# The layer norm's reciprocal root on VectorE (bit trick, two Newton steps) instead of ScalarE (Ln, Exp), with the planner's limits chosen anew

## The chip, the cores and the metric

The kernel runs on one core of one Trainium2 chip. Its engines work side by side and are named as the profile names them: PE (TensorE matmuls; PEld are its weight loads), ACT (ScalarE, the engine with the activation functions), DVE (VectorE), POOL (GpSimd) and SP (SyncE, which here only issues DMAs). The metric is the device time of one execution in microseconds; the median of the runs is compared. A profile is one execution, with every instruction's start and duration.

## The reference

Four layers stand one behind the other on an activation x of 2048 tokens by 512 features; there are 32 heads of 16 features. Layers 0 and 2 are of kind A, layers 1 and 3 of kind B.

```python
x = A_x
x = x + _A_ref(_layernorm(x), A_wq, A_wk, A_wv, A_wo, A_beta)
x = x + _B_ref(_layernorm(x), B_wqkv, B_wo)
x = x + _A_ref(_layernorm(x), A_wq, A_wk, A_wv, A_wo, A_beta)
x = x + _B_ref(_layernorm(x), B_wqkv, B_wo)

def _layernorm(x, eps=1e-05):
    m = mean(x, -1); v = var(x, -1)
    return (x - m) / sqrt(v + eps)
```

Kind A cuts the tokens into four segments of 512. Within a segment it is causal softmax attention; between segments a memory M (16 by 16 for each head) and a norm z are carried, read through phi(q) and written with phi(k), and a gate of beta mixes the two outputs. Kind B is full softmax attention over all 2048 tokens. Each ends in a product with wo and is added to x. So there are 16 normalisations of a segment (four layers by four segments), and in them one reciprocal root for each token: 512 numbers at a time, held as 128 partitions by 4.

## The kernel before

The kernel is laid down by a planner in Python that runs while the program is built. It keeps a model of when each engine will be free and writes the instructions of all five engines in the order that the model finds good; on the chip each engine then follows its own list and waits on semaphores.

**Units.** The main loop (`attention`, `unit`) takes the attention scores in banks of 128 keys by 512 queries, up to three to a unit. PE computes the scores of the banks (`ps<-qm,KB` and `ps<-qm,KA`), and one ACT instruction on line L1925 takes the exponential of all of a unit's banks from PSUM into `pT` in SBUF: 1536 columns for three banks, 1024 for two. PE multiplies `pT` by the values (`ps<-pT,VB`).

**Banks on VectorE.** When the planner thinks that ACT is behind, it gives one or two banks to DVE instead (`dx_open`, `ring_open`, `dx_first`). There an exponential is the sum of three approximations: line L1394 makes a 16-bit integer from the scores in PSUM, whose bits are read as bfloat16, and two more copies are made with an integer added (L1450 for two banks at once, L1493 for four, both on DVE; or L1475 on POOL). PE multiplies all three copies by the values, so a bank on DVE costs three such products and a bank on ACT one. The copies lie in `dxt` and in the buffers `KA`, `QA`, `VA`, `wA` and `wB` while these are not in use for their own data; in rows such as `KA<-ps 128x512 uint16` that name means such a bank.

**Background work.** Normalisations, projections, output products and memory updates are Python generators ("tasks") that the loop advances a step at a time between units. A task yields what it waits for, and how many PE columns and DVE nanoseconds the next step will cost; the loop runs a step when its credit allows it.

**Limits.** Every 20 units `set_limits` sets some 80 numbers from a row of the table `PLAN` (76 rows): from which lag of an engine a bank goes to DVE, when a copy goes to POOL, in which order background steps stand, how many matmuls with zeros are put into gaps of PE (`keep_busy`, `fill_gap`; the rows `ps<-woB,zero`).

**The normalisation** is `ln_part`: for each of a segment's four tiles of 128 tokens DVE computes mean and variance (`bn_stats`, `bn_aggr` into `lnst`). Then ACT makes the reciprocal root of the four variances in two small instructions: Ln with eps as bias on L882 and Exp with scale -0.5 on L885, both into `lnw` (128 by 4). The two are steps of their own; between them lies at least one unit. `normalize` (L895) then subtracts and multiplies on DVE into `xn`, and SP transposes `xn` into `xT` by DMA for the projections. The first segment of all goes through `ln_first` (L906), with transposes on PE and copies out of PSUM by ACT (L920) and DVE.

`setup` loads, before anything else, one activation table that holds both Ln and Exp (L825); Copy and Exp are the only other functions that ACT uses. `evac` copies a projection out of PSUM with DVE, or with ACT (L757) where the planner has ACT ahead of DVE by the limit EVAC_ACT.

Of the kernel before, what the change touches and what calls it, by code (L numbers as in the profile page):

```python
# [5 lines left out]
dt = mybir.dt  # L6
ACT = mybir.ActivationFunctionType
ALU = mybir.AluOpType
# [9 lines left out]
LN_EPS = 1e-5  # L18
LOG2E = 1.4426950408889634
# [397 lines left out]
class Builder:  # L417
# [5 lines left out]
        2: dict(FILL_DVE=400, MASK_PE=800, GAP=3, BG_BANK=400, QMIN=3, LOW=20, POOL_QM=1, ACT1=600, R_PAIRS=2, PE_LOW=7, DX_LATE=1700, DX_FIN=3000, OPART=3, HOLD_AT=12, PE_A=4, NEAR_A=50, TRADE=0, TAKEN_A=1, PART=3, DMA_LATE=700, CR_B=1200, SLACK=350, DMA_STEPS=0, POOL_WAIT=600, MARGIN=250, EVAC_ACT=1500),  # L423
        3: dict(R_LATE=1200, NEARW=40, PAIRS=999, MASK_PE=800, LEVEL=3, TAKEN=0.5, LOW=20, MARGIN=600, TAKEN_A=1, EARLY=300, OPART=3, QUAD=0, FILL=0.47, CR_A=1200, DX_LATE=700, CARRY_W=1500, PART=3, CR_W=2200, HOLD_MAX=0, DVE_LATE=1700, FILL_DVE=400, BUSY_WAIT=500, ACT1=300, QMIN=3, PE_LOW=7, PE_A=6, TRADE=400, DVE_LATE_LOW=2500, PACE=7, PE_B=6, ORD=3, POOL_WAIT=600),
        4: dict(R_LATE=1200, NEARW=40, PAIRS=999, MASK_PE=800, LEVEL=3, TAKEN=0.5, LOW=20, MARGIN=600, TAKEN_A=1, EARLY=300, OPART=0, QUAD=0, FILL=0.47, DX_BANK=900, CR_A=1200, DX_LATE=700, CARRY_W=1500, PART=3, CR_W=2200, HOLD_MAX=0, DVE_LATE=1700, FILL_DVE=400, BUSY_WAIT=500, ACT1=300, QMIN=3, PE_LOW=7, PE_A=6, TRADE=0, DVE_LATE_LOW=2500, POOL_D=2500, PACE=7, PE_B=6, POOL_MEM=0),
        5: dict(ACT1=300, NEAR=8, TAKEN_A=1, PV_SKIP=900, FILL_DVE=400, BACK=8, CR_W=2200, NEARW=40, OPART=0, TAKEN=0.4, LOW=20, DVE_LATE=800, QWAIT=8, HOLD_AT=40, PHI_LATE=0, REST=20, POOL_D=2500, R_LATE=1200, MARGIN=350, EARLY=300, QUAD=0, CR_A=1700, CARRY_W=1500, PART=3, BUSY_WAIT=500, PE_LOW=7, PE_A=6, HURRY=4000, PAIRS=999, LEVEL=3, DX_BANK=900, DX_LATE=700, QMIN=3, TRADE=0, DVE_LATE_LOW=2500, PACE=7, DVE_FIN=1500, MASK_PE=800, FILL=0.47),
        6: dict(ACT1=300, NEAR=8, TAKEN_A=1, PV_SKIP=900, FILL_DVE=400, BACK=8, CR_W=2200, NEARW=40, OPART=0, TAKEN=0.4, LOW=20, DVE_LATE=800, QWAIT=8, HOLD_AT=40, PHI_LATE=0, REST=20, POOL_D=2500, R_LATE=1200, MARGIN=350, EARLY=300, QUAD=0, CR_A=1700, CARRY_W=1500, PART=3, BUSY_WAIT=500, PE_LOW=7, PE_A=6, HURRY=4000, PAIRS=999, LEVEL=3, DX_BANK=900, DX_LATE=700, QMIN=3, TRADE=400, DVE_LATE_LOW=2500, PACE=7, DVE_FIN=1500, MASK_PE=800, FILL=0.47, DMA_LATE=0),
        7: dict(R_LATE=1200, NEARW=40, PAIRS=999, MASK_PE=800, LEVEL=3, TAKEN=0.4, LOW=20, MARGIN=350, TAKEN_A=1, EARLY=300, OPART=0, QUAD=0, FILL=0.47, DX_BANK=900, CR_A=1200, DX_LATE=700, CARRY_W=400, PART=3, CR_W=2200, HOLD_MAX=0, DVE_LATE=800, FILL_DVE=400, BUSY_WAIT=500, ACT1=300, DMA_LATE=0, GAP=3, QWAIT=8, NEAR=8, PE_A=6, POOL_QM=1, DVE_LATE_LOW=2500, PACE=7, DVE_FIN=200, HURRY=1500, PV_SKIP=900, POOL_D=2500, PE_LOW=7, QMIN=3),
        8: dict(R_LATE=1200, NEARW=40, PAIRS=999, MASK_PE=800, LEVEL=3, TAKEN=0.4, LOW=30, MARGIN=500, TAKEN_A=1, EARLY=500, OPART=0, QUAD=0, FILL=0.47, DX_BANK=900, CR_A=1200, DX_LATE=700, CARRY_W=1500, PART=3, CR_W=2200, DVE_LATE=1700, FILL_DVE=400, BUSY_WAIT=500, ACT1=300, DMA_LATE=0, QWAIT=8, NEAR=8, PV_SKIP=900, NEAR_A=0, HURRY=1500, QMIN=3),
        9: dict(MARGIN=600, NEAR=3, PV_SKIP=200, FILL_DVE=100, BUSY_ROOM=900, FILL=0.4, CR_W=1500, CARRY_W=400, R_PAIRS=2, OPART=4, GAP=3, DVE_LATE=800, QMIN=1, HOLD_AT=40, POOL_QM=1, ACT1=300, DX_LATE=900, REST=8, CR_B=1800, DX_LAG=1, BACK=6, LOW=14, BUSY_WAIT=500, POOL_D=1200, PART=3, PHI_LATE=0, EVAC_ACT=100, RUSH0=40, AHEAD=1000, RUSH=120, DX_TAIL=300, FIT=3),  # L430
        10: dict(ACT1=200, MARGIN=600, R_LATE=2200, EVAC_ACT=800, NEAR=10, CR_W=1300, CR_B=1800, R_PAIRS=2, DIV_LATE=800, TAKEN=0.5, DVE_LATE=800, BG_BANK=400, PHI_LATE=300, OPART=3, NEARW=20, POOL_C=2000, DX_LAG=1, POOL_D=1200, REST=12, EARLY=500, POOL_QM=1, DX_FIN=3000, DMA_LATE=1200, PE_LOW=7, HOLD_SEGS=2, PV_SKIP=200, QUAD=0, LN1_AT=6, FILL_DVE=400, QMIN=4, BUSY_WAIT=0, PORT_FREE=150, DX_LATE=700),
        11: dict(ACT1=200, NEAR=10, PV_SKIP=200, EARLY=500, FILL=0.53, CR_B=1800, CARRY_W=400, OPART=2, MASK_PE=800, DIV_LATE=800, BG_BANK=100, QUAD=0, LN1_AT=6, FILL_DVE=400, R_LATE=1500, POOL_C=4000, QMIN=4, POOL_D=1200, DVE_LATE=1700, DX_FIN=3000, POOL_QM=1, DVE_FIN=1500, PE_A=4, SPARE=20, PACE=7, MARGIN=600),
        12: dict(MARGIN=600, NEAR=10, PV_SKIP=100, FILL_DVE=200, BUSY_ROOM=300, FILL=0.53, CR_W=1500, CARRY_W=400, R_PAIRS=2, OPART=2, GAP=3, DVE_LATE=800, QMIN=1, POOL_QM=1, PAIRS=999, SLACK=350, R_NEAR=10, CR_B=1800, QWAIT=8, LN1_AT=6, CR_A=1200, POOL_D=2500, POOL_WAIT=0, POOL_C=2000, PACE=7, MASK_PE=800, ACT1=300, RATE=2, REST_A=20, CR_LOW=4000, PART=0, LEVEL=3, BG_BANK=100, QUAD=0, R_LATE=1500, PE_A=4, SPARE=20),
        13: dict(MARGIN=600, NEAR=10, PV_SKIP=100, FILL_DVE=200, BUSY_ROOM=300, FILL=0.55, CR_W=1500, CARRY_W=400, R_PAIRS=2, OPART=2, GAP=3, DVE_LATE=800, QMIN=1, POOL_QM=1, PAIRS=999, SLACK=350, R_NEAR=10, CR_B=1800, QWAIT=8, LN1_AT=6, CR_A=1200, POOL_D=2500, POOL_WAIT=0, POOL_C=2000, PACE=7, MASK_PE=800, ACT1=300, RATE=2, REST_A=20, CR_LOW=4000, PART=0, BG_BANK=100, QUAD=0, R_LATE=1500, PE_A=4, SPARE=20, DX_BANK=900),
# [64 lines left out]
    MASK_PE = 500  # L499
    MASK_POOL = 2000  # L500
    PHI_LATE = 100
    POOL_MEM = 1500
# [3 lines left out]
    NEARW = 60  # L506
# [358 lines left out]
    def ln_part(self, L, s):  # L865
# [14 lines left out]
        if not first:  # L880
            yield [("free", [bw], self.b_lnst[k])], 0, 0
        self.op("act", lambda e: e.activation(v, var, ACT.Ln, bias=self.eps[:, 0:1]), reads=self.b_lnst[k] + [self.b_eps], writes=[bw], ns=341, gap=250)  # L882
        if not first:
            yield [("at", self.step + 1)], 0, 0
        self.op("act", lambda e: e.activation(y, v, ACT.Exp, scale=-0.5), reads=[bw], writes=[bw], ns=236, gap=200)  # L885
        if first:
            self.parity()
# [1478 lines left out]
```

## Time and profile before

| | before |
|---|---|
| runs | 1660.08, 1660.99, 1661.16 us; median 1660.99 us |
| profiled execution | 1660.92 us, of which its span (first to last instruction) is 1659.2 us |
| ACT busy | 1622.0 us, 98% of the span, 1575 instructions |
| PE busy | 1573.7 us, 95% |
| DVE busy | 1397.2 us, 84% |
| POOL busy | 1227.6 us, 74% |
| granted TensorE clock, mean | 0.999 |

Busy time is the time in which at least one instruction of the engine (or of the group) was under way. Instructions of ACT overlap a little: the next starts some 0.1 us before the one ahead has ended, so the distance from one start to the next is shorter than the duration. In the rows, "idle before" is the time in which the engine had nothing under way just ahead of the group, followed by what ended it.

### The profile page before, as it was taken

What the parts mean: (1) busy time and instruction counts of PE and PEld (TensorE: products, weight loads), DVE (VectorE), ACT (ScalarE), POOL (GpSimd) and SP (SyncE); (2) the same over time, 40 slices, a digit from 0 to 9 for tenths busy, and PEclk for the clock granted to TensorE, in tenths of its full rate; (3) what the DMA queues carried; (4) which work ended last, traced back from release to release, by engine and by line L of the source; (5) the groups of instructions that cost most, each with busy time, mean ns of one, the idle gap of its engine ahead of it and who ended that gap; (6) DMA issues with size and microseconds to landing.
All of it is one profiled execution on the core that took longest, in us unless ns stands there. A gap on an engine that the chain in (4) does not pass through costs nothing.

```text
span 1659.2 us, 45418 instructions
## 1 busy us (share of the span) xinstructions
PE 1573.7 (95%) x19667; PEld 568.6 (34%) x19738; DVE 1397.2 (84%) x2232; ACT 1622.0 (98%) x1575; POOL 1227.6 (74%) x1322
## 2 busy tenths in 40 slices
PE   8999999999999999999999999999999999999998
PEld 5553435222222535222235222442222222222236
DVE  5668666979998687899878997779899999999996
ACT  7999999999999999999999999999999999999998
POOL 3342234779898443699875898577899999999995
PEclk9999999999999999999999999999999999999999
DMA  6211211001120322200212102112001200100000
GB/s 185 41 21 26 40 27 28 8 8 30 23 62 11 72 68 43 58 11 14 58 24 31 49 14 55 18 21 53 1 14 24 46 11 11 27 11 11 22 16 19
DMA packets 148424, 54.46 MB, mean 33 GB/s; under 512 B 128768, under 2 KB 147712, under 8 KB 148224
## 3 DMA queue, kind: packets, MB, share of 16 engines
q1 hardware_dynamic: 148224, 51.56, 14.8%
q8 instruction: 154, 2.52, 0.7%
q14 instruction: 46, 0.38, 0.1%
HBM read 18.88 MB, written 2.10 MB: 13 GB/s over the span
## 4 chain that ended last, share of the span: by engine, by line
ACT 60%; PE 25%; DVE 9%; DMA 2%; POOL 2%; issue 1%; SPq 0%; ACTq 0%; POOLq 0%
ACT pT L1925 59%; PE ps L683 24%; DVE KA L1394 2%; DVE dxt L1394 1%; ACT amem L966 1%; DVE wA L1394 1%; DVE wB L1394 1%; DMA tb<-ub 1%; DMA xT<-xn 1%; DMA phq<-amem 1%; DMA phk<-KA 0%; SPq L766 0%; POOL pT L1939 0%; DVE lnst L873 0%; DVE xn L895 0%
## 5 line engine op out<-in xcount | busy, mean ns | idle before, releaser
L1925 ACT ACTIVATE pT<-ps 128x1024 bf16<-128x1024 f32 (+1 forms) x1503 | 1592.0, 1230 | 21.0 <-PE ps L683 18.1
L683 PE MATMUL ps<-qm,KB 32*128 32x512 bf16 x4096 | 543.9, 385 | 53.3 <-ACT pT L1925 39.0
L683 PE MATMUL ps<-pT,VB 128*17 128x512 bf16 x2751 | 476.7, 384 | 1.6 <-DVE dxt L1394 0.7
L1475 POOL TENSOR_TENSOR dxt<-dxt,shift 128x512 int32<-128x512 int32 (+1 forms) x293 | 312.8, 1079 | 103.2 <-DVE dxt L1394 73.3
L1394 DVE TENSOR_SCALAR KA<-ps 128x512 uint16<-128x512 f32 (+1 forms) x438 | 339.3, 793 | 24.1 <-PE ps L683 21.7
L683 PEld LDWEIGHTS ps<-qm,KB 32*128 32x128 bf16 x4096 | 139.4, 91 | 558.7 <-ACT pT L1925 442.5
L1394 DVE TENSOR_SCALAR dxt<-ps 128x512 uint16<-128x512 f32 (+1 forms) x332 | 257.3, 789 | 27.3 <-PE ps L683 25.7
L1475 POOL TENSOR_TENSOR QA<-KA,shift 128x512 int32<-128x512 int32 x208 | 227.3, 1103 | 53.4 <-DVE KA L1394 52.9
L683 PE MATMUL ps<-dxt,VB 128*17 128x512 bf16 x1125 | 249.8, 381 | 0.3 <-POOL dxt L1475 0.3
L683 PEld LDWEIGHTS ps<-pT,VB 128*17 128x17 bf16 x2751 | 111.0, 87 | 272.8 <-issue 257.4
L1475 POOL TENSOR_TENSOR VA<-KA,shift 128x512 int32<-128x512 int32 x172 | 184.7, 1083 | 24.0 <-DVE QA L1450 18.5
L1939 POOL TENSOR_SCALAR_AFFINE_SELECT pT<-pT 128x512 bf16<-128x512 bf16 (+4 forms) x135 | 71.7, 546 | 170.7 <-ACT pT L1925 170.4
L1475 POOL TENSOR_TENSOR wA<-wA,shift 128x512 int32<-128x512 int32 (+1 forms) x140 | 151.8, 1096 | 9.8 <-DVE wA L1394 6.4
L683 PE MATMUL ps<-QA,VB 128*17 128x512 bf16 x499 | 145.6, 381 | 0.0
L683 PE MATMUL ps<-VA,VB 128*17 128x512 bf16 x499 | 143.6, 381 | 0.0
L1475 POOL TENSOR_TENSOR wB<-wB,shift 128x512 int32<-128x512 int32 x114 | 124.0, 1102 | 5.9 <-DVE wB L1394 4.3
L683 PE MATMUL ps<-KA,VB 128*17 128x512 bf16 x499 | 127.6, 381 | 0.0
L1394 DVE TENSOR_SCALAR wA<-ps 128x512 uint16<-128x512 f32 (+1 forms) x150 | 120.6, 817 | 8.2 <-PE ps L683 7.3
L683 PE MATMUL ps<-wA,VB 128*17 128x512 bf16 x558 | 125.4, 381 | 0.0
L1394 DVE TENSOR_SCALAR wB<-ps 128x512 uint16<-128x512 f32 (+1 forms) x128 | 103.7, 823 | 4.9 <-PE ps L683 4.7
L683 PE MATMUL ps<-VA,pT 128*128 128x51 bf16 (+1 forms) x2488 | 103.0, 187 | 1.4 <-POOL pT L1939 0.6
L683 PE MATMUL ps<-wB,VB 128*17 128x512 bf16 x471 | 104.2, 381 | 0.0
(174 smaller groups left out, 2061.6 us busy)
## 6 DMA issues: line engine op xcount, KB each, us to landing
wB<-in_B_wqkv_dram SPq DMA_DIRECT2D x48, 128.0 KB, 2.4
wA<-in_A_wk_dram SPq DMA_DIRECT2D x16, 128.0 KB, 2.4
wA<-in_A_wq_dram SPq DMA_DIRECT2D x16, 128.0 KB, 2.6
wA<-in_A_wv_dram SPq DMA_DIRECT2D x16, 128.0 KB, 2.8
out_dram<-x SPq DMA_DIRECT2D x8, 256.0 KB, 2.2
x<-in_A_x_dram SPq DMA_DIRECT2D x3, 512.0 KB, 9.7
wB<-in_B_wqkv_dram SPq DMA_DIRECT2D x1, 1536.0 KB, 12.8
oT<-ob SPq DMA_TRANSPOSE x63, 2.5
```

Of the source, the lines that this page charges most:

```text
L683: self.sc.add("pe", lambda e: e.matmul(out, lhsT, rhs, start=start, stop=stop, skip_group_check=True), reads=reads, banks=[(bank, "w", all ...
L966: self.op("act", lambda e: e.activation(et, src, ACT.Exp), reads=bsrc, writes=self.b_amem, ns=1023, gap=915)
L1394: self.op("dve", lambda e: e.tensor_scalar(d, o, SCALE * LOG2E * 128, 127.0 * 128 + EXP_BIAS, op0=ALU.mult, op1=ALU.add), writes=self.b_dx ...
L1475: self.op("pool", lambda e: e.tensor_tensor(d, s, c, ALU.add), reads=src + [self.b_shift] + [first] * k, writes=dst, ns=165 + 1.75 * n, ga ...
L1925: self.sc.add("act", (lambda dst, src: lambda e: e.activation(dst, src, ACT.Exp, scale=SCALE))(dst, src), writes=self.b_pT[slot * 3 + i:sl ...
L1939: self.op("pool", (lambda blk, pat: lambda e: e.affine_select(blk, blk, pattern=pat, compare_op=ALU.is_ge, fill=0.0, base=0, channel_multi ...
```

## The change

Segment (0, 0), the first of all: ACT computes Sqrt of the variance plus eps instead of Ln, and DVE takes the reciprocal; an Exp of one column of the constant eps follows on ACT, whose result is not used. The other fifteen segments: ACT does nothing; DVE adds eps, forms a first value by reading the bits as an integer, multiplying by -0.5 and adding a constant, and makes two Newton steps of three instructions each, all on 128 by 4 elements of `lnw`. The explicit table load of `setup` is gone; loads come where the functions need them. 49 of the 76 rows of `PLAN` have other numbers; one of them is shown.

```diff
+RSQRT_MAGIC = 1597463007.0
...
-        2: dict(..., CR_B=1200, SLACK=350, DMA_STEPS=0, POOL_WAIT=600, MARGIN=250, EVAC_ACT=1500),
+        2: dict(..., CR_B=1200, SLACK=550, DMA_STEPS=2, POOL_WAIT=600, MARGIN=250, EVAC_ACT=1500),
...
-        self.sc.add("act", lambda e: e.preload_act_table_set("natural_log_exp_and_others"), ns=1283, gap=1283)
...
         bw = self.b_lnw[k]
-        v, y = w[:, k, 0, :], w[:, k, 1, :]
+        yield [], 0, 400
+        v, y, tt = w[:, k, 0, :], w[:, k, 1, :], w[:, k, 2, :]
         var = st[:, k, :, 7]
-        first = (L, s) == (0, 0)
-        if not first:
-            yield [("free", [bw], self.b_lnst[k])], 0, 0
-        self.op("act", lambda e: e.activation(v, var, ACT.Ln, bias=self.eps[:, 0:1]), reads=self.b_lnst[k] + [self.b_eps], writes=[bw], ns=341, gap=250)
-        if not first:
-            yield [("at", self.step + 1)], 0, 0
-        self.op("act", lambda e: e.activation(y, v, ACT.Exp, scale=-0.5), reads=[bw], writes=[bw], ns=236, gap=200)
-        if first:
+        if (L, s) == (0, 0):
+            self.op("act", lambda e: e.activation(v, var, ACT.Sqrt, bias=self.eps[:, 0:1]), reads=self.b_lnst[k] + [self.b_eps], writes=[bw], ns=230)
+            self.op("act", lambda e: e.activation(self.eps[:, 1:2], self.eps[:, 0:1], ACT.Exp), reads=[self.b_eps], writes=[self.b_eps], ns=1500)
             self.parity()
+            self.op("dve", lambda e: e.reciprocal(y, v), reads=[bw], writes=[bw], ns=165)
+            return k
+        self.op("dve", lambda e: e.tensor_scalar(v, var, LN_EPS, None, op0=ALU.add), reads=self.b_lnst[k], writes=[bw], ns=165)
+        vi, yi = v.bitcast(dt.int32), y.bitcast(dt.int32)
+        self.op("dve", lambda e: e.tensor_scalar(yi, vi, -0.5, RSQRT_MAGIC, op0=ALU.mult, op1=ALU.add), reads=[bw], writes=[bw], ns=165)
+        for it in range(2):
+            yield [], 0, 560
+            self.op("dve", lambda e: e.scalar_tensor_tensor(tt, y, -0.5, y, op0=ALU.mult, op1=ALU.mult), reads=[bw], writes=[bw], ns=165)
+            self.op("dve", lambda e: e.tensor_tensor(tt, tt, v, ALU.mult), reads=[bw], writes=[bw], ns=165)
+            self.op("dve", lambda e: e.scalar_tensor_tensor(y, tt, 1.5, y, op0=ALU.add, op1=ALU.mult), reads=[bw], writes=[bw], ns=165)
         return k
```

Since the planner decides by its model and its limits, the order of the instructions is another from the second segment on. In the lists below the lines of the changed kernel are up to 6 higher for the same work (L1925 is L1931 there). Three places follow.

ACT at the start of the program, before: one table load on L825, then Ln, Exp and the copy of the first `xT`.

```order
L825 ACT_TABLE_LOAD
L829 ACTIVATE ps<-zero 128x512 x2
L882 ACTIVATE lnw<-lnst,eps 128x4
L885 ACTIVATE lnw<-lnw 128x4
L920 ACTIVATE xT<-ps 128x4x256
```

The same place in the changed kernel:

```order
L829 ACT_TABLE_LOAD
L829 ACTIVATE ps<-zero 128x512 x2
L881 ACT_TABLE_LOAD
L881 ACTIVATE lnw<-lnst,eps 128x4
L882 ACT_TABLE_LOAD
L882 ACTIVATE eps<-eps 128x1
L926 ACTIVATE xT<-ps 128x4x256
```

Two more table loads stand there, one ahead of Sqrt and one ahead of the Exp that nobody reads.

DVE around the normalisation of the second segment (0, 1), before (`rd` and `ob` are the division of a finished attention group, `KA` and `QA` copies of projections):

```order
L873 BN_STATS lnst<-x 128x6
L875 BN_AGGR lnst<-lnst 128x2
L759 CAST QA<-ps 128x512
L2037 RECIPROCAL rd<-ps 128x16
L2043 TENSOR_TENSOR ob<-ps,rd 128x16x16
L759 CAST KA<-ps 128x512
L895 TENSOR_SCALAR xn<-x,lnst,lnw 128x512 x2
```

The same place in the changed kernel:

```order
L873 BN_STATS lnst<-x 128x6
L875 BN_AGGR lnst<-lnst 128x2
L886 TENSOR_SCALAR lnw<-lnst 128x4
L888 TENSOR_SCALAR lnw<-lnw 128x4
L760 CAST QA<-ps 128x512
L891 SCALAR_TENSOR_TENSOR lnw<-lnw 128x4
L892 TENSOR_TENSOR lnw<-lnw 128x4
L893 SCALAR_TENSOR_TENSOR lnw<-lnw 128x4
L891 SCALAR_TENSOR_TENSOR lnw<-lnw 128x4
L892 TENSOR_TENSOR lnw<-lnw 128x4
L893 SCALAR_TENSOR_TENSOR lnw<-lnw 128x4
L901 TENSOR_SCALAR xn<-x,lnst,lnw 128x512
```

Eight small instructions stand between the last variance and the first `xn`; one copy of a projection and one division stand elsewhere.

ACT in the last stretch before the end of the program, before:

```order
L1925 ACTIVATE pT<-ps 128x1024 x5
L1925 ACTIVATE pT<-ps 128x1536
L1925 ACTIVATE pT<-ps 128x1024 x7
L1925 ACTIVATE pT<-ps 128x1536
L1925 ACTIVATE pT<-ps 128x1024 x6
L1925 ACTIVATE pT<-ps 128x1536
L1925 ACTIVATE pT<-ps 128x1024 x12
L1925 ACTIVATE pT<-ps 128x1536 x4
L1274 ACTIVATE oT<-ps 128x256
```

The same place in the changed kernel:

```order
L1931 ACTIVATE pT<-ps 128x1536
L1931 ACTIVATE pT<-ps 128x1024 x3
L1931 ACTIVATE pT<-ps 128x1536
L1931 ACTIVATE pT<-ps 128x1024 x4
L1931 ACTIVATE pT<-ps 128x1536
L1931 ACTIVATE pT<-ps 128x1024 x15
L1931 ACTIVATE pT<-ps 128x1536
L1931 ACTIVATE pT<-ps 128x1024 x13
L1931 ACTIVATE pT<-ps 128x1536 x3
L1931 ACTIVATE pT<-ps 128x512
L1280 ACTIVATE oT<-ps 128x256
```

The mixture of units of three and of two banks is another, and the last unit holds one bank. Counted over the whole list of each engine, the two programs differ so:

| instructions | before | changed |
|---|---|---|
| ACT exponentials of 1536, 1024, 512 columns | 453, 1050, 0 | 483, 1022, 1 |
| the same in banks of 512 | 3459 | 3494 |
| ACT Ln, Exp (Sqrt, Exp) of the normalisation | 16, 16 | 1, 1 |
| ACT copies of 512 columns out of PSUM by `evac` | 7 | 10 |
| ACT table loads | 1 | 3 |
| DVE first pass of a bank: 512, 1024 columns | 819, 229 | 802, 220 |
| the same in banks of 512 | 1277 | 1242 |
| DVE second and third copy: 1024, 2048 columns | 203, 74 | 152, 88 |
| DVE on `lnw` | 0 | 121 |
| POOL copies of 512 int32 columns | 917 | 902 |
| PE value products of 512 columns from banks on DVE | 3651 | 3540 |
| PE value products of 512 columns from `pT` | 2751 | 2788 |
| PE matmuls with zeros | 337 | 390 |

98 lines of the change are left out of this document (49 added, 49 removed).

## Prediction

> **What bounds the kernel now.** I read the page's busy times and chain first, then a table by stretches, then the waits of the engine that these name.
>
> ```profile
> PE 1573.7 (95%) x19667; PEld 568.6 (34%) x19738; DVE 1397.2 (84%) x2232; ACT 1622.0 (98%) x1575; POOL 1227.6 (74%) x1322
> ACT 60%; PE 25%; DVE 9%; DMA 2%; POOL 2%; issue 1%; SPq 0%; ACTq 0%; POOLq 0%
> ```
>
> ```profile
> 0.00:20.00 20.00, 15.11 (x193) 10.23 (x195) 11.70 (x32) 10.35 (x15) 5.41 (x21) 1.00 0.89 297
> 200.00:300.00 100.00, 93.03 (x1342) 41.88 (x1346) 66.94 (x124) 96.81 (x83) 46.84 (x65) 0.98 0.15 23
> 1200.00:1300.00 100.00, 96.26 (x1016) 25.83 (x1014) 94.82 (x136) 99.74 (x103) 96.38 (x95) 1.00 0.12 23
> 1500.00:1600.00 100.00, 95.21 (x1020) 25.56 (x1017) 97.65 (x128) 99.69 (x105) 99.41 (x94) 1.00 0.08 18
> 1600.00:1659.00 59.00, 54.17 (x1121) 32.54 (x1120) 45.11 (x70) 52.40 (x55) 39.71 (x36) 0.99 0.06 16
> ```
>
> The columns of the second fence are: stretch, its length, then busy us of PE, PEld, DVE, ACT and POOL, then the granted clock. ACT is busy for 1622.0 of 1659.2 us, and idle for 37.2. Of these 9.65 lie in the first 20 us (20 - 10.35) and 6.6 in the last 59. The rest, some 21 us, is spread over 1580 us, and from 1200 on there is almost nothing: 0.3 us in each hundred. PE's 95% is no second bound of the same kind, since its wait for scores' banks ends with ACT (the page's chain runs through ACT for 60%). What ACT waits for between the ends is one thing:
>
> ```profile
> ACT pT L1925 <- PE ps L683: 17.3, 43, 1.4
> ```
>
> That is the list of waits from 20 to 1630 us: 17.3 us in 43 waits. So the time is ACT's work, plus 16 us at the two ends, plus about 20 us of waiting in between. A change is worth what it adds to or takes from the work of ACT, unless it also changes that waiting.
>
> **The price of ACT's instructions.** Since they overlap, start-to-start distances count and not durations.
>
> ```profile
> 162.24 1.48 ACT L1925 ACTIVATE pT<-ps 128x1536 bf16<-128x1536 f32 x1
> 163.57 0.24 ACT L885 ACTIVATE lnw<-lnw 128x4 f32<-128x4 f32 x1
> ...
> 811.93 0.31 ACT L882 ACTIVATE lnw<-lnst,eps 128x4 f32<-128x4 f32 x1
> 812.12 1.04 ACT L1925 ACTIVATE pT<-ps 128x1024 bf16<-128x1024 f32 x1
> 813.02 0.23 ACT L885 ACTIVATE lnw<-lnw 128x4 f32<-128x4 f32 x1
> 813.12 2.38 ACT L1925 ACTIVATE pT<-ps 128x1536 bf16<-128x1536 f32 x2
> ```
>
> Ln takes 812.12 - 811.93 = 0.19 us of ACT, Exp 813.12 - 813.02 = 0.10. An exponential of 1024 columns takes 813.02 - 812.12 = 0.90, one of 1536 columns 163.57 - 162.24 = 1.33. The same from two stretches with hardly any other form in them (18 of 1536 columns; 34 instructions, of which the first and the last are of 1536 columns and cut by the edges, so 32 of 1024):
>
> ```profile
> 1213.95:1243.25 29.30, 29.30 (x34) 1.00 0.10 20
> 644.20:668.20 24.00, 24.00 (x18) 1.00 0.25 41
> ```
>
> 29.30 / 32 = 0.916 and 24.00 / 18 = 1.333. I take these; a bank more in a unit then costs 1.333 - 0.916 = 0.417 us, and a unit of one bank 0.916 - 0.417 = 0.50.
>
> **Term 1, the small instructions on ACT.** Fifteen pairs of Ln and Exp go: 15 x 0.29 = 4.35 us less. The sixteenth pair is exchanged for Sqrt and an Exp of the same kind and size or smaller: 0.
>
> **Term 2, the banks.** The number of banks is fixed by the attention (3459 + 1277 = 3494 + 1242 = 4736), but the changed program gives ACT 35 more of them: 30 more exponentials of 1536 columns, 28 fewer of 1024 and one of 512. That is 30 x 1.333 - 28 x 0.916 + 0.50 = 40.0 - 25.65 + 0.5 = +14.85 us. This is the price of the room that the Newton steps take on DVE, and it is the largest term. DVE's own account, from its rows (the first two are banks' first pass of 512 and 1024 columns, the next two copies for two and for four banks, then the nearest row to an instruction of 128 by 4):
>
> ```profile
> L1394 DVE TENSOR_SCALAR KA<-ps 128x512 uint16<-128x512 f32 x347 | 231.6, 681 | 16.2 <-PE ps L683 14.6
> L1394 DVE TENSOR_SCALAR KA<-ps 128x1024 uint16<-128x1024 f32 x91 | 111.1, 1221 | 8.0 <-PE ps L683 7.2
> L1450 DVE TENSOR_SCALAR dxt<-dxt 128x1024 uint16<-128x1024 uint16 x68 | 39.8, 588 | 1.1
> L1493 DVE TENSOR_SCALAR VA<-KA 128x2048 uint16<-128x2048 uint16 x29 | 27.0, 929 | 0.2
> L1089 DVE TENSOR_TENSOR Mz<-M,hmask 128x8 bf16<-128x8 f32 x19 | 3.5, 182 | 0.0
> ```
>
> The 120 Newton instructions cost 120 x 0.182 = 21.8 us. Banks take away 17 x 0.681 + 9 x 1.221 = 22.6, copies 51 x 0.588 - 14 x 0.929 = 17.0. DVE ends with some 18 us less, POOL with 15 copies less, so neither becomes the bound; they are not what is scarce. The cover of the Newton steps themselves is DVE's idle time: all 15 chains fall before the last normalisation, which ended before 1140 us, and the table has DVE at 67 to 95 in a hundred there. I cost them at nothing directly. If that cover is gone, as in a stretch at 95, a chain of 8 delays its `xn` by 8 x 0.18 = 1.5 us, against 0.29 of ACT and the unit between before; queued behind it on DVE are banks of L1394, and PE waits for those. Before, `xn` waited itself:
>
> ```profile
> DVE xn L895 <- ACT lnw L885: 7.2, 9, 1.6
> ```
>
> These 7.2 us of DVE go. They were beside ACT's work and are worth nothing on the path.
>
> **Term 3, copies by ACT.** Three more projections or results are copied out of PSUM by ACT (10 for 7). A copy has 512 columns, as the unit of one bank has: 3 x 0.50 = +1.5 us.
>
> **Term 4, the start.** Two table loads more stand on ACT.
>
> ```profile
> 0.80 1.28 ACT L825 ACT_TABLE_LOAD   x1 [0.80 <-PEq L2351]
> 2.17 1.12 ACT L829 ACTIVATE ps<-zero 128x512 f32<-128x512 bf16 x2
> 6.28 0.30 ACT L882 ACTIVATE lnw<-lnst,eps 128x4 f32<-128x4 f32 x1 [2.99 <-DVE par L836]
> 6.61 0.20 ACT L885 ACTIVATE lnw<-lnw 128x4 f32<-128x4 f32 x1
> 8.08 1.02 ACT L920 ACTIVATE xT<-ps 128x1024 bf16<-128x1024 bf16 x1 [1.26 <-PE ps L730]
> ```
>
> The first of the two stands ahead of Sqrt with no wait of its own, so it fits into the 2.99 us in which ACT has nothing. The second follows Sqrt at 6.6: 6.6 + 1.28 + 0.2 for the Exp on eps = 8.1, where the copy of `xT` began at 8.08. DVE's reciprocal takes the place of ACT's Exp ahead of `xn` (0.18 for 0.20). I take +0.1. The bounds are 0 and both loads in full, 2.6.
>
> The Trainium skill (ScalarE: Activation LUTs, What ACT_TABLE_LOAD costs) gives a switch of set as 1283 ns of load and about 1380 ns of drain behind it. The trace agrees on the load (1.28 us in the row) and shows no drain: the copy starts at 2.17, 0.09 us after the load's end at 2.08. By that rule of the Trainium skill the second load would end 1.4 us later, the copy of `xT` with it, and the sum below would be 1674.4; by the row it is 1673.0, and the row decides.
>
> **Term 5, ACT's waiting.** No row shows the waits of another order. The bounds come from the 17.3 us: all of them gone, or as many again. I take no change. Behind the choice: with 35 banks fewer on DVE PE has 111 - 37 = 74 value products of 512 columns less, which lets scores come earlier, and 53 more matmuls with zeros, which only fill what PE leaves free.
>
> **Sum.** -4.35 + 14.85 + 1.5 + 0.1 = +12.1 us against the profiled execution's 1660.92: 1673.0 us. That execution lies 0.07 below the median of 1660.99, which changes nothing at this precision. The bounds of the terms put together run from 1673.0 - 17.3 = 1655.7 to 1673.0 + 2.5 + 17.3 = 1692.8.
>
> **Rivals.**
>
> Faster, because the new limits take out ACT's waits. Place: units between 20 and 1100 us where scores come late. It needs more than 12.1 of the 17.3 us, 70% of them, only to stand level, and at 15.4 it is faster by what can be told apart. If all goes, the time is 1655.7. For it: the waits are many and small (43 with a longest of 1.4), so order alone can remove them. Against it: ACT's banks are added, so each wait must go although ACT, not DVE, is asked for more; and from 1200 us on there is nothing to win.
>
> No change that can be told apart: half to nine tenths of the waits go (8.8 to 15.4 us). The time is 1657.7 to 1664.2. For and against as above. A related case is that the added banks sit in units that waited for PE anyway; then the same 17.3 us are the limit, and it is counted here.
>
> Slower still, because the granted clock of PE drops more often. It happened once before:
>
> ```profile
> 280.00:290.00 10.00, 8.90 (x125) 4.33 (x126) 6.42 (x11) 7.21 (x7) 7.01 (x10) 0.83 0.17 36
> ```
>
> In these 10 us the clock is 0.83 on average and ACT is busy for 7.21: 2.8 us lost in one event. PE now has less real work in its gaps (the 74 products) and needs more filling with zeros (390 for 337), so it is nearer to such an event. Three more cost 8.4 us: 1681.4. Against it: the planner fills for this purpose, and one event in 1660 us is rare.
>
> **How the numbers follow.** A difference of 0.2% (3.3 us) is about what a measurement of this kernel can tell from none. My forecast, 1673.0 with its own range of 1666 to 1680, has 0.68. The clock rival (1680 to 1690) has 0.10. Slower with part of the waits gone (1664.3 to 1666) has 0.07. No change has 0.09, faster 0.06. So faster 0.06, same 0.09, slower 0.85. The range is 1664 to 1682: it leaves out about 0.14 below and 0.05 above.
>
> **What would show it.** Term 1 and 2: ACT's groups on the exponential line with 483 of 1536 columns and 1022 of 1024, together 16 to 17 us more busy time (busy time is somewhat larger than the distances), and no `lnw` on ACT beyond the first. Term 4: the first `xT` copy on ACT at 8.1 us, and no idle time of 3 us ahead of Sqrt that starts behind a load. Term 5: ACT's waits for PE between 20 us and 30 us before the end near 17 us; below 5 the forecast is wrong on the low side, above 27 on the high side. Clock: at most one stretch below 1.00 between the ends. DVE's busy time near 1397 - 18 = 1379 us. The prediction falls if ACT's work grows as counted and its idle time shrinks by the same amount.

## The result, and the profile after

The changed kernel is slower: 1680.22, 1687.30 and 1688.14 us, median 1687.3, a ratio of 1.0147 to before with the interval [1.0105, 1.0190]. The direction was forecast, the size was not: 1687.3 lies above the range of 1664 to 1682. The runs of one program differ with the granted clock (1680.22 us at a mean clock of 1.000, 1688.14 at 0.997), so below each kernel is compared with before in the same job, by the ratio.

The profiled execution of the changed kernel is the one of 1680.22 us, with a span of 1678.5 us and the clock at 1.000. The page's busy times and its chain, in the same columns as before:

```profile
PE 1578.7 (94%) x19614; PEld 566.8 (34%) x19684; DVE 1392.6 (83%) x2287; ACT 1638.5 (98%) x1553; POOL 1217.8 (73%) x1331
ACT 61%; PE 26%; DVE 6%; POOL 3%; DMA 2%; issue 1%; ACTq 0%; DVEq 0%; POOLq 0%
```

ACT still sets the time: 98% busy and 61% of the chain. ACT's two largest groups, shapes kept apart:

```profile
L1931 ACT ACTIVATE pT<-ps 128x1024 bf16<-128x1024 f32 x1022 | 978.1, 1112 | 7.7 <-PE ps L684 6.3
L1931 ACT ACTIVATE pT<-ps 128x1536 bf16<-128x1536 f32 x483 | 688.2, 1507 | 18.1 <-PE ps L684 16.7
```

The counts are those of the order, and the mean of one instruction is what it was (1112 and 1507 ns, before 1110 and 1508). ACT's wait for scores, 20 us to 1650 us:

```profile
ACT pT L1931 <- PE ps L684: 20.6, 53, 1.5
```

Before it was 17.3 us in 43 waits, from 20 us to 1630 us. The start of ACT:

```profile
0.80 1.28 ACT L829 ACT_TABLE_LOAD   x1 [0.80 <-PEq L2357]
2.17 1.12 ACT L829 ACTIVATE ps<-zero 128x512 f32<-128x512 bf16 x2
3.31 1.28 ACT L881 ACT_TABLE_LOAD   x1
6.27 0.30 ACT L881 ACTIVATE lnw<-lnst,eps 128x4 f32<-128x4 f32 x1 [1.68 <-DVE par L836]
6.59 1.28 ACT L882 ACT_TABLE_LOAD   x1
7.88 0.20 ACT L882 ACTIVATE eps<-eps 128x1 f32<-128x1 f32 x1
8.04 1.02 ACT L926 ACTIVATE xT<-ps 128x1024 bf16<-128x1024 bf16 x1
```

The copy of `xT` begins at 8.04, before at 8.08: both extra loads lie in time that ACT had free. The first stretch of the table by time (columns as in the prediction: PE, PEld, DVE, ACT, POOL, clock):

```profile
0.00:20.00 20.00, 14.70 (x195) 9.82 (x197) 11.88 (x33) 12.91 (x17) 5.42 (x21) 1.00 0.89 297
```

From these rows the 19.3 us that the span grew (1678.5 - 1659.2) can be split. ACT's busy time grew by 16.5 us (1638.5 - 1622.0). Some 2.6 of it are the two loads, which only fill the first 20 us: idle time there fell from 9.65 to 20 - 12.91 = 7.09. So ACT's work outside the start grew by 13.9 us; the prediction had 12.0 for it. ACT's idle time outside the first 20 us was 37.2 - 9.65 = 27.5 and is 1678.5 - 1638.5 - 7.1 = 32.9: +5.4. The prediction had 0 for it. 13.9 + 5.4 = 19.3. Most of the 5.4 is the wait for scores, which over the whole span went from 18.1 to 23.0 us: from 4.1 to 7.8 us between 20 and 200 us, from 0.3 to 2.0 in the last 30 us, and from 13.2 to 12.7 in all the time between.

### The profile page after: what moved, and what is told of

Read it like the earlier page. It is cut to its first block, busy times and chain, and to the rows that moved or that the text cites. A ratio compares the mean times of both kernels' runs of the same rounds, so it can differ in the third digit from the quotient of the medians.

```text
span 1678.5 us, 45367 instructions
## 1 busy us (share of the span) xinstructions
PE 1578.7 (94%) x19614; PEld 566.8 (34%) x19684; DVE 1392.6 (83%) x2287; ACT 1638.5 (98%) x1553; POOL 1217.8 (73%) x1331
## 4 chain that ended last, share of the span: by engine, by line
ACT 61%; PE 26%; DVE 6%; POOL 3%; DMA 2%; issue 1%; ACTq 0%; DVEq 0%; POOLq 0%
ACT pT L1931 60%; PE ps L684 26%; DVE dxt L1400 1%; POOL wB L1481 1%; ACT amem L972 1%; DVE KA L1400 1%; POOL wA L1481 1%; DMA phq<-amem 1%; POOL dxt L1481 0%; DVE wB L1400 0%; DMA xT<-xn 0%; DVE lnst L873 0%; POOL VA L1481 0%; POOL QA L1481 0%; DVE wA L1400 0%
## 5 line engine op out<-in xcount | busy, mean ns | idle before, releaser
L1931 ACT ACTIVATE pT<-ps 128x1024 bf16<-128x1024 f32 (+1 forms) x1506 | 1605.6, 1238 | 25.8 <-PE ps L684 23.0
L1400 DVE TENSOR_SCALAR KA<-ps 128x512 uint16<-128x512 f32 (+1 forms) x392 | 301.1, 788 | 29.4 <-PE ps L684 27.1
L1481 POOL TENSOR_TENSOR QA<-KA,shift 128x512 int32<-128x512 int32 x193 | 210.2, 1098 | 95.4 <-DVE KA L1400 95.2
L1945 POOL TENSOR_SCALAR_AFFINE_SELECT pT<-pT 128x256 bf16<-128x256 bf16 (+4 forms) x152 | 79.6, 538 | 173.0 <-ACT pT L1931 172.6
L1481 POOL TENSOR_TENSOR VA<-KA,shift 128x512 int32<-128x512 int32 (+1 forms) x169 | 177.8, 1062 | 10.2 <-DVE QA L1456 3.0
L1481 POOL TENSOR_TENSOR wA<-wA,shift 128x512 int32<-128x512 int32 (+1 forms) x157 | 167.2, 1079 | 18.8 <-DVE wA L1400 16.2
L1400 DVE TENSOR_SCALAR wA<-ps 128x512 uint16<-128x512 f32 (+1 forms) x172 | 139.7, 827 | 10.3 <-PE ps L684 8.6
L684 PE MATMUL ps<-wA,VB 128*17 128x512 bf16 x636 | 143.5, 381 | 0.3 <-POOL wA L1481 0.2
L684 PE MATMUL ps<-QA,VB 128*17 128x512 bf16 x442 | 129.8, 381 | 0.0
L684 PE MATMUL ps<-VA,VB 128*17 128x512 bf16 x442 | 122.2, 381 | 0.1
## 6 DMA issues: line engine op xcount, KB each, us to landing
wB<-in_B_wqkv_dram SPq DMA_DIRECT2D x1, 1536.0 KB, 13.4
```

Of the source, the lines that this page charges most:

```text
L684: self.sc.add("pe", lambda e: e.matmul(out, lhsT, rhs, start=start, stop=stop, skip_group_check=True), reads=reads, banks=[(bank, "w", all ...
L1400: self.op("dve", lambda e: e.tensor_scalar(d, o, SCALE * LOG2E * 128, 127.0 * 128 + EXP_BIAS, op0=ALU.mult, op1=ALU.add), writes=self.b_dx ...
L1481: self.op("pool", lambda e: e.tensor_tensor(d, s, c, ALU.add), reads=src + [self.b_shift] + [first] * k, writes=dst, ns=165 + 1.75 * n, ga ...
L1931: self.sc.add("act", (lambda dst, src: lambda e: e.activation(dst, src, ACT.Exp, scale=SCALE))(dst, src), writes=self.b_pT[slot * 3 + i:sl ...
L1945: self.op("pool", (lambda blk, pat: lambda e: e.affine_select(blk, blk, pattern=pat, compare_op=ALU.is_ge, fill=0.0, base=0, channel_multi ...
```

## The experiments

Two theories stood at the beginning. **Theory A**: the price is the new order that the new limits make (more banks on ACT, other waits), and the Newton steps themselves are covered by DVE's idle time, as the prediction says. **Theory B**: the price is the Newton steps, which hold up what stands behind them in DVE's list.

**The changed kernel again, in more runs.** No edit.

> The changed kernel unchanged, timed five more times. It had 1680.2, 1687.3 and 1688.1 us with mean granted clocks of 1.000, 0.998 and 0.997. If the upper two come from drops of the granted TensorE clock, each execution's time follows its clock: about 1680 us at a clock of 0.999 or more, and some 3 us more for each 0.001 below. If the spread has another cause, times and clocks don't go together.

1681.31 us (1679.71 at a clock of 1.000 to 1684.15 at 0.997), ratio 1.0126 [1.0113, 1.0139]. That is +21 us. The slower executions of the first three were those with the lower clock; about 20 us are there with a clock of 1.000. The clock goes with the time here too, but 0.003 less of it went with 4.4 us more, half of what was expected.

**The Newton steps without the new order.** The planner runs as before with Ln and Exp; when the order is complete, the fifteen pairs are taken off ACT and eight instructions are put on DVE, right ahead of the first `xn` of the segment. All else has the order of before, instruction for instruction.

```diff
+            first = next(i for i, o in enumerate(ops["dve"]) if two in o.deps)
...
+                ops["act"].remove(one)
+                ops["act"].remove(two)
+            ops["dve"][first:first] = made
```

> The order of the kernel before, instruction for instruction, but the fifteen pairs of Ln and Exp are taken from ACT and the eight Newton instructions of each segment stand on DVE right ahead of the segment's first xn. The planner doesn't know of it. Theory A (the loss is the new order with its 35 banks more on ACT and its waits, the exchange itself is a small gain): -4.35 us for the pairs and up to +2 for delays, 1656.5 to 1659 us, ACT busy about 1613 us. Theory B (eight dependent instructions on DVE, 1.5 us and more, delay xn, banks and copies, and ACT waits for it): 15 x 0.5 to 15 x 1.5 us more, 1664 to 1680 us, ACT waits for PE of 25 us and more.

1673.48 us, ratio 1.0081 [1.0067, 1.0095]: +13.4 us, although 35 banks did not move and ACT has less to do. Theory B held here. One chain, on DVE:

```profile
186.44 0.17 DVE L2330 TENSOR_SCALAR lnw<-lnst 128x4 f32<-128x4 f32 x1
...
187.83 0.16 DVE L2335 SCALAR_TENSOR_TENSOR lnw<-lnw 128x4 f32<-128x4 f32 x1
188.03 0.74 DVE L899 TENSOR_SCALAR xn<-x,lnst,lnw 128x512 bf16<-128x512 bf16 x2
188.68 0.69 DVE L761 CAST VB<-ps 128x512 bf16<-128x512 f32 x1
```

The eight take 1.55 us. Behind them stand `xn` and then a copy of a projection out of PSUM into `VB`. PE, and then ACT, in the same piece:

```profile
187.75 0.48 PE L685 MATMUL ps<-VA,pT 128*128 128x51 bf16 x12
189.42 1.04 PE L685 MATMUL ps<-wB,xT 128*128 128x512 bf16 x4 [1.20 <-DVE VB L761]
190.39 0.40 PE L685 MATMUL ps<-qm,KA 32*128 32x128 bf16 x10
```

```profile
188.18 1.47 ACT L1929 ACTIVATE pT<-ps 128x1536 bf16<-128x1536 f32 x1
190.86 2.79 ACT L1929 ACTIVATE pT<-ps 128x1536 bf16<-128x1536 f32 x2 [1.21 <-PE ps L685]
```

PE's next projection (`ps<-wB,xT`) waits 1.20 us for the `VB` copy. The scores (`ps<-qm,KA`) stand behind the projection in PE's list, and ACT waits 1.21 us for them. In the trace of before ACT runs through the same place without a wait:

```profile
183.53 1.08 ACT L966 ACTIVATE amem<-QA 128x1024 bf16<-128x1024 bf16 x1
184.48 4.15 ACT L1925 ACTIVATE pT<-ps 128x1536 bf16<-128x1536 f32 x3
```

In this trace a gap in PE is also followed by a second cost, a drop of the clock. Behind the last chain (1145 us), from the table by tens of us of this kernel:

```profile
1140.00:1150.00 10.00, 7.93 (x99) 2.31 (x99) 9.12 (x27) 7.89 (x8) 2.94 (x4) 0.90 0.10 20
1150.00:1160.00 10.00, 10.00 (x70) 1.82 (x67) 7.04 (x11) 7.56 (x9) 6.34 (x7) 0.59 0.62 165
```

PE is idle for 2.1 us in the first stretch, then granted 0.59 of its clock, and ACT is busy for only 7.56 of 10.

The 1503 exponentials of ACT stand in the same order in this trace and in that of before, so they can be compared one by one. In the profiled execution (1676.66 us) they are 5.0 us late at 200 us, behind five chains; 7.6 us late at 1000 us, behind twelve; and 15.6 us late at 1200 us, behind all fifteen. So the price is no equal sum for each chain: the last three, around which the clock drops, make half of it.

**Less work and nothing for it.** The same order; the pairs leave ACT and nothing replaces them (the reciprocal root is left out).

```diff
+                ops["act"].remove(one)
+                ops["act"].remove(two)
```

> The order of the kernel before; the fifteen pairs of Ln and Exp leave ACT and nothing takes their place (xn is made with what stands in lnw: the root is left out for all segments but the first). This is the removal alone. Theory C (the removal gives what ACT's rows say, the loss of the exchange is what the Newton steps do on DVE): -4.35 us and no new waits, 1655 to 1657 us. If the pairs were covered by ACT's waits for PE: 1659 to 1661 us.

1657.29 us, ratio 0.9977 [0.9968, 0.9986]: -3.8 by the ratio, -3.3 by the medians. Term 1 had -4.35. So the gain from taking the pairs off ACT is about 3.5 us in this order, if nothing else gets slower.

**The chain earlier.** The eight instructions stand right behind the last variance instead of right ahead of `xn`, so that `xn` waits for nothing.

```diff
-            first = next(i for i, o in enumerate(ops["dve"]) if two in o.deps)
+            first = max(i for i, o in enumerate(ops["dve"]) if o in one.deps) + 1
```

> As the run with the Newton steps in the order of before (1673.5 us), but each chain of eight stands right behind the segment's last variance, several DVE instructions ahead of the first xn. Theory C1 (what costs is that xn, and with it the transposes and projections, comes later): the chain is done before xn is due, 1656 to 1660 us. Theory C2 (what costs is that 1.55 us are put into DVE's list, so that whatever stands behind comes later, and PE's list with it): 1666 to 1674 us, with a wait of 0.5 to 2 us of ACT behind each chain.

1685.82 us, ratio 1.0153 [1.0135, 1.0170]: +25, worse than both expected. So it isn't the delay of `xn` alone that costs, but that of whatever stands behind the chain in DVE's list; this held for both places that were tried. The mean clocks of its runs were 0.989 to 0.994, so a part of the +25 is the clock.

**The chain besides Ln and Exp.** ACT keeps the pairs and `xn` uses their root; the eight instructions are extra work on DVE, right ahead of `xn`, which waits for both.

```diff
+                ops["dve"][first].deps.append(last)
...
+            ops["dve"][first:first] = made
```

> The order of before with Ln and Exp left on ACT and used; the same eight Newton instructions stand ahead of each segment's first xn as extra work whose result goes to a tile of its own. DVE's addition alone. If removal and addition add up: the 1673.5 us of the exchange plus 4.35, 1676 to 1680 us. If the chains cost only because xn had no other work to wait for (the wait for Exp covers them here): 1661 to 1668 us.

1676.11 us, ratio 1.0096 [1.0080, 1.0113]: +15.9 us, on average 1.06 us for each of fifteen chains. With the -3.8 of the kernel without a root the sum is +12.1, and the exchange measured +13.4: within their intervals gain and price simply add.

**A shorter chain.** As the second experiment, but with one Newton step, so five instructions instead of eight (0.97 us for 1.55; the root is less exact).

```diff
-            for _ in range(2):
+            for _ in range(1):
```

> The order of before with Ln and Exp off ACT and only one Newton step on DVE, so a chain of 5 instructions in place of 8 (the root is less exact). A clean chain of eight took 1.55 us, so five take 0.97. Theory B in its proportional form (what DVE's list is held up by passes on to ACT by a fixed share, found from 13.5 + 3.3 us for 15 chains of 1.55 us: 16.8 / 23.3 = 0.72): 15 x 0.97 x 0.72 - 3.3 = +7.2 us, 1666 to 1669. Rival P (the price is one event for each chain, whatever its length, such as a wait that is missed once or a drop of the clock): +12 to +14 us, 1671 to 1675. Rival S (only what goes beyond DVE's gaps counts, and five instructions mostly fit in them): +0 to +3 us, 1660 to 1663.

1665.0 us, ratio 1.0027 [1.0015, 1.0040]: +4.5 us, between Theory B in its proportional form (+7.2) and rival S (up to +3), and outside the ranges of both. The rival of one price for every chain is out. Above the kernel without a root it is 8.3 us, on average 0.55 for each chain of 0.97 us; for eight instructions it is 13.4 + 3.8 = 17.2, or 1.15 for each chain of 1.55. So the last 0.58 us of a chain cost 0.60 on average, the first 0.97 only 0.55. That looks like a gap of 0.4 us ahead of each chain with all beyond passed on in full, but the traces don't bear it out. Compared one by one with before, the exponentials of the kernel with five instructions are 2.6 us late at 200 us, 1.3 at 1000 and 4.5 at 1200: the seven chains between 200 and 1000 us cost nothing with five instructions and 2.6 us in all with eight. And at the one mean clock that both kernels had (0.998: 1665.5 against 1671.38 and 1672.18) the last 0.58 us cost some 0.4 for each chain, so a part of the 0.60 comes with the lower clocks of the longer chain.

**The chain on POOL.** Ten instructions (the three-operand form is written as two) in POOL's list, where the planner had Ln.

```diff
-            ops["dve"][first:first] = made
+            ops["pool"][first:first] = made
```

> The order of before, Ln and Exp off ACT, the root by the bit trick and two Newton steps on POOL instead of DVE (10 instructions of 128 x 4, since the three-operand form is written as two), placed in POOL's list where the planner had Ln. DVE, PE and SP have the order of before. Theory Q (it is DVE's list that must not be held up: what stands behind the chain there feeds PE at once): POOL's list is emptier before 1140 us, its holding up costs little, and the time is 1657 to 1661, at or below before. Theory R (any list that is held up by 1.5 to 2 us passes it on to PE and ACT): about 1 us for each of 15 chains as on DVE, 1668 to 1675.

1678.22 us, ratio 1.0109 [1.0094, 1.0125]: +18 us. Theory Q is out: another in-order list passes the delay on too. But the time lies 3 us above the range of Theory R, with mean clocks of 0.991 to 0.994. The chain holds POOL for longer than its ten instructions, since the first waits for the variance, from POOL's groups (idle time and its releaser last):

```profile
L2330 POOL TENSOR_SCALAR lnw<-lnst 128x4 f32<-128x4 f32 x15 | 3.4, 224 | 17.2 <-DVE lnst L877 16.4 <-POOL dxt L1479 0.2 <-POOL lnw L2336 0.2
```

16.4 us in eight waits. So this run doesn't separate the chain's own length on POOL from that wait. ACT's wait for scores in the kernels with the order of before, without a root, with five, with eight, and with eight early instructions on DVE, and on POOL (one line each, whole span):

```profile
ACT pT L1929 <- PE ps L685: 18.8, 48, 1.7
```

```profile
ACT pT L1929 <- PE ps L685: 25.1, 57, 1.5
```

```profile
ACT pT L1929 <- PE ps L685: 35.0, 65, 2.7
```

```profile
ACT pT L1929 <- PE ps L685: 41.3, 70, 3.7
```

```profile
ACT pT L1929 <- PE ps L685: 35.9, 53, 4.7
```

In this one row the price can be read directly: from 18.8 to 25.1 and 35.0 us as the chain grows, while ACT's busy time is nearly the same in all five (1618.5 to 1621.6 us).

**The new order without the Newton steps.** The changed kernel's order; afterwards the fifteen chains are taken out of DVE and Ln and Exp put back on ACT.

```diff
+            ops["act"].insert(at, ln)
+            ops["act"].insert(at + 2, ex)
+            for o in made:
+                ops["dve"].remove(o)
```

> The order of the changed kernel, but the Newton instructions are taken from DVE and Ln and Exp stand on ACT, each pair as early as the planned times of the variances allow and one exponential apart; one table load as before. Theory A: 4.35 us more than the changed kernel at the same clock, 1684 us where that has 1680. Theory B: at least 8 us less than the changed kernel, 1672 us or below.

1684.0 us, ratio 1.0139 [1.0126, 1.0152]: 2.7 us above the changed kernel's 1681.31 of its own five rounds. Here Theory A held: where the planner knew of the steps, exchanging them for Ln and Exp gives nothing back; 2.7 us more were measured. The order alone, with no Newton step in it, carries the whole loss. The page's busy times:

```profile
PE 1581.6 (94%) x19614; PEld 567.8 (34%) x19684; DVE 1370.5 (81%) x2166; ACT 1640.2 (98%) x1581; POOL 1217.9 (72%) x1331
```

DVE is 22.1 us less busy than in the changed kernel (1392.6), and the time is no shorter for it.

**Limits and code apart.** First the code of before with the new limits, then the changed code with the limits of before.

```diff
-        2: dict(..., CR_B=1200, SLACK=350, DMA_STEPS=0, POOL_WAIT=600, MARGIN=250, EVAC_ACT=1500),
+        2: dict(..., CR_B=1200, SLACK=550, DMA_STEPS=2, POOL_WAIT=600, MARGIN=250, EVAC_ACT=1500),
```

> The code of the kernel before (Ln and Exp on ACT) with the changed kernel's table of limits, planned anew. Counted in its list: 507 exponentials of 1536 columns and 1004 of 1024, that is 54 x 1.333 - 46 x 0.916 = +29.8 us of ACT's work against the kernel before, and two copies more (+1.0). If the limits and the order that comes of them make the time: 1660.9 + 31 = 1692 us, and more where the clock drops (481 matmuls with zeros for 337). If the Newton steps make it: near 1661 us.

1723.37 us, ratio 1.0373 [1.0357, 1.0388].

> The changed kernel's code with the limits of before. It has 497 exponentials of 1536 columns, 1008 of 1024 and one of 512, 12 more copies by ACT. Counted, ACT's work is 44 x 1.333 - 42 x 0.916 + 0.50 - 4.35 + 12 x 0.50 = +22.3 us. Theory A of the prediction (work counts, waits stay): 1683. Theory L (limits that were not fitted to an order cost waits as well, as the code of before with the new limits did: 25 us more than counted): 1690 to 1715.

1745.1 us, ratio 1.0521 [1.0502, 1.0541]. Against the counts (1692 and 1683) these are 31 and 62 us more; the second is 30 us beyond what Theory L had. Its mean clocks were 0.990 to 0.995, so a part of that is the clock. ACT's wait for scores in the first and the second:

```profile
ACT pT L1925 <- PE ps L683: 42.0, 84, 4.0
```

```profile
ACT pT L1931 <- PE ps L684: 59.7, 85, 5.1
```

A table of limits belongs to the code for which it was found. Exchanged, it gave ACT more banks both times and let it wait more besides. The second result also says what the new limits do in the change: the changed code takes 1745 us with the limits of before and 1681 with its own.

**The same search for both codes.** For each of the two codes limits were searched anew, on the planner's side alone and with the same effort. All rows of `PLAN` may differ; one of them, in the changed kernel and in its searched form:

```diff
-        40: dict(ACT1=200, ..., FILL=0.4, ..., ORD=3, CR_A=1200),
+        40: dict(R_LATE=1200, ..., FILL=0.47, ..., RGAP=1, PORT_FREE=900, DX_LAG=2, HOLD_SEGS=1, R_PAIRS=1),
```

> The changed kernel's code with a third set of limits, found by a search in which this code and the code of before got the same effort. It gives ACT 436 exponentials of 1536 columns and 1085 of 1024: 3478 banks, 19 more than before and 16 fewer than the changed kernel; 7 more copies by ACT than before. Counted as in the prediction, ACT's work is -17 x 1.333 + 35 x 0.916 - 4.35 + 7 x 0.50 = +8.6 us against before. Theory L (the 35 banks belong to how well the limits fit, not to the room of the Newton steps): 1660 + 8.6 + 0 to 7 of waits = 1668 to 1676, level with or below the kernel that keeps Ln and Exp and got the same search. Theory N (the steps need room on DVE that only 35 banks can give): with 16 banks of that room given back DVE's copies come late, ACT's waits grow by what the banks save, and it stays at 1681 or above, 8 us or more over its sister.

> The code of before (Ln and Exp on ACT) with limits found by the same search. It has 472 exponentials of 1536 columns and 1036 of 1024: 3488 banks on ACT, 29 more than before although no Newton step takes room on DVE. Counted, ACT's work is 19 x 1.333 - 14 x 0.916 - 0.50 = +12.0 us. Theory L: 1660 + 12 + 0 to 7 = 1672 to 1679, within 5 us of the Newton kernel with searched limits. Theory N: 8 us or more below that kernel.

Newton steps: 1682.07 us, ratio 1.0128 [1.0113, 1.0143], 3478 banks on ACT. Ln and Exp: 1680.36 us, ratio 1.0121 [1.0106, 1.0136], 3488 banks on ACT. They can't be told apart, so Theory N (8 us or more between them) is out, although the Newton kernel stayed above 1681 as that theory had it; the code with Ln and Exp gives ACT even 10 banks more. Theory L was right on that and wrong on the size: the Newton kernel lies 6 us above what was expected, its sister 1. ACT's exponentials with the Newton steps, then its wait for scores there and in the kernel with Ln and Exp:

```profile
L1931 ACT ACTIVATE pT<-ps 128x1024 bf16<-128x1024 f32 x1085 | 1034.0, 1097 | 11.2 <-PE ps L684 8.9
L1931 ACT ACTIVATE pT<-ps 128x1536 bf16<-128x1536 f32 x436 | 620.6, 1501 | 17.9 <-PE ps L684 16.5
```

```profile
ACT pT L1931 <- PE ps L684: 25.5, 57, 2.6
```

```profile
ACT pT L1925 <- PE ps L683: 22.9, 53, 2.5
```

The Newton kernel has 16 banks fewer on ACT than the changed one and is not faster; its waits are longer: ACT is 3.1 us less busy (1635.4) and 4.9 us more idle. Neither search came near the limits of before (1660), so this shows that the two codes are alike at this effort, not what the best limits of either would give. No kernel of the study beat before with its whole computation.

## Why the prediction missed

The direction was right. The step that failed is Term 5, ACT's waiting, which the sum put at no change and which measured +5.4 us; and the sum had nothing for executions with a lower clock, which make the other half of the distance to the median.

**Right: what bounds the kernel, terms 1, 3 and 4.** ACT set the time before and after, and its busy time grew by 16.5 us, as forecast (16 to 17). Term 1 measured -3.3 to -3.8 alone, for -4.35. A copy by ACT takes 0.48 to 0.49 us from its start to the next start where no wait follows, for 0.50 in Term 3. Term 4 came out as the row of before said: the second load ends at 6.59 + 1.28 = 7.87 and the next instruction starts at 7.88, the copy of `xT` at 8.04 (8.1 was forecast). The drain that the Trainium skill names (ScalarE: Activation LUTs, What ACT_TABLE_LOAD costs) doesn't appear in this trace either.

**Right in size, wrong in its reason: Term 2.** The work of ACT outside the start grew by 13.9 us where terms 1 to 3 had 12.0. But "the price of the room that the Newton steps take on DVE" was only argued. The searched kernels speak against it: with the Newton steps 3478 banks are on ACT, without them 3488. So the number of banks goes with the limits, and with them the order; nothing here shows that the steps need the room.

**Wrong: Term 5, "I take no change".** ACT's idle time outside the start grew by 5.4 us in the profiled execution, for the most part in waits for scores between 20 and 200 us (+3.7) and in the last 30 us (+1.7). The range allowed for this at its upper end, but the choice of the middle leaned on fewer value products on PE, a sum over the whole program that says nothing on when a single score is ready. The mark of 27 us for the waits, above which the forecast would be wrong, was not reached by that execution (20.6), and it still lay 7 us over the forecast: 1.9 from work, 5.4 from idle time.

**Wrong in its reason, nearly right in size: "I cost them at nothing directly".** DVE at 67 to 95 in a hundred is no sure cover, because its list is in order: an idle moment later doesn't help the copy that stands behind the chain now. In the order of before the chains cost 17 us in all, 1.1 us for each on average. The prediction named the path (banks and PE behind the chain) and the length (1.5 us), and then left the price out of the sum and out of the range. In the changed kernel, whose planner knew of the steps, they cost some 1 us in all, if Ln and Exp are worth there what they are in the order of before (3.8 - 2.7, each with an interval of about 2 us to either side). They aren't broken up for this: ten of the fifteen chains run in one piece there. The waits between 20 and 200 us are 5.8 us in the same order without the steps, for 7.8 with them; one of the waits behind a chain is shown in the last section. The loss came with the new order, but the searched kernel with Ln and Exp lost as much (1680.36), so it is not shown that it is a price of the steps.

**Partly come true: the clock rival.** It had a chance of 0.10. The profiled execution has a clock of 1.000, so it isn't the cause of the 19.3 us. But two of the first three runs had 0.998 and 0.997 and took 7 to 8 us more, and the median is one of them: of the 14.3 us between the forecast and 1687.3, half is work and idle time (7.2), the other half (7.1) the difference between two executions of one program. That the clock makes all of this half is not shown; in the repeat 0.997 went with 4.4 us. The executions with a clock of 1.000 (1679.71 to 1680.9) lie within the range at its upper end, and the median of the repeat, 1681.31, does too, by 0.7 us; the forecast is 7 us low even for them.

What one drop costs can be read from two profiled executions of the changed kernel, the first one and that of the repeat, in the same 10 us:

```profile
80.00:90.00 10.00, 8.29 (x141) 4.81 (x141) 5.37 (x12) 8.49 (x9) 3.53 (x6) 1.00 0.37 54
80.00:90.00 10.00, 8.50 (x122) 4.94 (x121) 4.61 (x11) 7.42 (x8) 2.46 (x5) 0.83 0.27 42
```

ACT is 1.1 us less busy where the clock is 0.83, and the whole span is 1.5 us longer (1680.0 for 1678.5). The prediction had 2.8 us for one drop, since it put all of ACT's idle time in such a stretch down to the clock; here 1.5 us of it are there with a clock of 1.00 too.

**DVE's own account.** The Newton steps were sized well (22.6 us by their groups, 21.8 forecast):

```profile
L893 DVE SCALAR_TENSOR_TENSOR lnw<-lnw 128x4 f32<-128x4 f32 x30 | 5.8, 194 | 1.0
L892 DVE TENSOR_TENSOR lnw<-lnw 128x4 f32<-128x4 f32 x30 | 5.3, 178 | 1.0
L891 DVE SCALAR_TENSOR_TENSOR lnw<-lnw 128x4 f32<-128x4 f32 x30 | 5.3, 178 | 0.9
L886 DVE TENSOR_SCALAR lnw<-lnst 128x4 f32<-128x4 f32 x15 | 3.1, 208 | 0.3
L888 DVE TENSOR_SCALAR lnw<-lnw 128x4 int32<-128x4 int32 x15 | 3.1, 206 | 0.5
```

DVE's total is 1392.6, not 1379: the copies for two and four banks fell by 8.3 us where 17.0 were forecast, and the rest wasn't followed up. DVE is still not the bound.

**What stays open.** Which of the new order's decisions cost the 5.4 us of idle time was not isolated, though the places are known. Why the clock drops in some executions of one program and not in others is not explained by these runs, and no trace was taken of an execution at 1687 us.

## What to carry to other kernels

An engine's idle share alone is no cover for a new instruction, and the price differs from place to place: look at what stands right behind it in that engine's list, who waits for that, and what stands behind the waiter in its own list. When a change comes with a newly planned order, count the work by the order, and take for the waits a loss rather than no change, since here every newly planned order raised them (22.9 to 59.7 us over the whole span, for 18.1). To judge the code apart from the order, freeze the order of one kernel and exchange only the code in it.

## What the runs showed of the hardware

A small DVE instruction can be held until a POOL instruction ends. Of the 120 Newton instructions of the changed kernel eight take more than 0.3 us, and each of the eight ends within 0.03 us of the end of a POOL instruction. One of them, at 80 us, with what follows on PE and ACT:

```profile
80.15 0.16 DVE L892 TENSOR_TENSOR lnw<-lnw 128x4 f32<-128x4 f32 x1
80.28 0.86 POOL L1945 TENSOR_SCALAR_AFFINE_SELECT pT<-pT 128x768 bf16<-128x768 bf16 x1 [0.98 <-ACT pT L1931]
80.35 0.81 DVE L893 SCALAR_TENSOR_TENSOR lnw<-lnw 128x4 f32<-128x4 f32 x1
...
81.36 0.42 DVE L2049 TENSOR_TENSOR ob<-ps,rd 128x256 bf16<-128x256 f32 x1
81.84 0.79 PEld L684 LDWEIGHTS ps<-VA,pT 128*128 128x128 bf16 x28 [0.99 <-DVE ob L2049]
...
82.21 1.45 ACT L1931 ACTIVATE pT<-ps 128x1536 bf16<-128x1536 f32 x1 [1.50 <-PE ps L684]
```

The last Newton instruction takes 0.81 us instead of 0.16 and ends at 81.16, POOL's at 81.14; the division behind it (`ob`) is late, PE's next weight load waits 0.99 us for it and ACT 1.50 us for PE. The Trainium skill (SBUF — State Buffer, SBUF: two separate sides) says that DVE and GpSimd share a port pair which one of them holds for its whole instruction, among others when a DVE operation with two inputs in SBUF meets a GpSimd operation that reads SBUF; this trace agrees, with the two ends 0.02 us apart.
